# Last row pair of a token-mixing layer: an addition moved into the PSUM bank of C21, and the seven products in another order

## The chip, the cores and the metric

The kernel runs on one core of one Trainium2 chip. The time is the device time of one execution in microseconds; the number shown for a kernel is the median of its runs. A core has five engines with a queue each, which run side by side and wait for one another: TensorE (PE, matrix products, with its weight loads shown apart as PEld), VectorE (DVE), ScalarE (ACT), GpSimd (POOL) and SyncE (SP, here an issuer of transfers). Products go into PSUM, eight banks, and are read from there by VectorE or ScalarE.

## What is computed

A sum of three terms on a token matrix of 2048 rows and 640 columns: the input itself, the real part of a two-dimensional Fourier transform of its layer norm, and a token-mixing MLP on that layer norm, normalized once more.

```
xn = _layernorm(x, axis=-1)
return x + _A_ref(xn, A_dft_seq_re, A_dft_seq_im, A_dft_hid_re, A_dft_hid_im) + _B_ref(xn, B_w1, B_b1, B_w2, B_b2)

# _B_ref
h = _layernorm(x, axis=-1)                       # (B, S, D)
u = jnp.einsum("bsd,sf->bdf", h, w1) + b1        # (B, D, F)
u = _gelu(u)
y = jnp.einsum("bdf,fs->bds", u, w2) + b2        # (B, D, S)
```

S is 2048, D is 640, F is 1728. All is in float32. The change lies in the last 9 us, at the end of the product with w2, whose result is added to what the output rows hold already.

## The kernel before

**Stages.** The kernel runs through the Fourier product over the sequence (columns, TensorE lines 496 and 656), the product over the hidden dimension ("hid"), the first MLP product ("up0", "up1") and the second ("down0", "down1"). Every stage from "hid" on is made of row pairs, by `row_steps`. A row pair of "down1" computes output rows of tiles t and t + 8, each 128 x 640, over one half of F. The last is t = 7.

**Seven products.** A row pair is a 2 x 2 block product by seven products instead of eight (the Winograd form of Strassen's method). The weights' blocks A11, A12, A21, A22 and sums of them are the stationary operands; the other factor, already cut and summed, is the moving one, 320 columns wide. The sums are s = A21 + A22 (`first_sum`), then s - A11 (`s2`), A21 = A11 - A21 (`s3`), A12 = A12 - s (`s4`), all on VectorE (lines 877 and 149). P1 takes A11, P5 takes s as first summed, P6 takes s after s2, P2 takes A12, P7 takes A21 after s3, P3 takes A12 after s4, P4 takes A22. The results are C11 = P1 + P2, C12 = P1 + P6 + P5 + P3, C22 = P1 + P6 + P7 + P5 and C21 = P1 + P6 + P7 + P4. PSUM bank z holds the running sum P1, P1 + P6, P1 + P6 + P7; bank y holds P5, P5 + P3; bank w holds P2. In other row pairs P4 too accumulates in z. In the last one before the change it gets a bank of its own, u.

**Three matmuls for one.** An operand is cut into a high half, rounded to float32r by ScalarE (line 143, tile `piece`), and the rest, the low half, which VectorE computes (line 146). `three` (lines 151 to 157) issues high x high, high x low and low x high, so line 157 is the first to need the low half. In "down1" a product has three blocks of 128; P2, P3 and P4 are "stacked": their last block has only 64 rows, its low half lies in the other 64, and it takes two matmuls. Such a product has 8 matmuls, the others 9. A stacked low half is two VectorE operations. `fourth` (line 996, ScalarE) copies the 64 rows of A12 anew after s4 has changed them. The cut pieces lie in three buffers by turns, so the high half of a product waits until the product three places before has been done.

**Order.** Each engine's queue is in the order of the program. Turn i (`turn_of`) issues: loads, `reads` (the readers of the product of turn i - 1), `sums`, the high half of step i + 2, `extras`, the low half of step i + 2, `behind_lo`, and last the products of step i. So in a queue the reader of a product stands at the start of the next turn, behind all that earlier turns put there. A reader on VectorE adds the bank to the tile c (lines 952 and 961); P1's is a copy on ScalarE (line 965). Waits between engines on the same tile or bank are placed by the framework.

**The last row pair.** `base` is there: the old output rows are loaded beforehand into a tile (line 1136), VectorE adds them (lines 961, 978, 982, and what P4's reader finds in c), and the results go out by plain transfers (`each`, line 1128), on SP's queue and, for C21's right half, on ScalarE's. Other row pairs add to the output by GpSimd transfers (line 1038). Before the change P3's reader is followed by C11 plus its old output, P7's reader by c = z + old output of C21, and P4's reader adds bank u to that in two halves of 160 columns, both on VectorE, each sent as soon as it is done.

Of the kernel before, what the change touches and what calls it, by code (L numbers as in the profile page):

```python
# [11 lines left out]
AF = mybir.ActivationFunctionType  # L12
# [15 lines left out]
H2 = D // 2  # L28
# [42 lines left out]
def fnet_plus_mixer(  # L71
# [30 lines left out]
    nc = tc.nc  # L102
# [45 lines left out]
    def sub(to, a, b):  # L148
        nc.vector.tensor_sub(to, a, b)  # L149
# [20 lines left out]
    loads, sums, reads, extras, timed, behind_lo = (defaultdict(list) for _ in range(6))  # L170
# [683 lines left out]
    def row_steps(stage, nq, load_piece, at, end, bias=(None, None), base=None, earliest=0, each=None, aside={}, tail=False, stacked=()):  # L854
# [6 lines left out]
        s0, n = len(steps), nq * P  # L861
        raw, banks, held = {}, {}, {}
# [19 lines left out]

        order = (1, 5, 2, 6, 3, 7, 4) if base else (1, 5, 6, 2, 7, 3, 4)

        early = n < D
        loads_of = {-6: ("A11", "A21", "A22"), -4: ("A12",)} if early else {
# [9 lines left out]
        bank_of = {1: "z", 6: "z", 7: "z", 4: "z", 5: "y", 3: "y", 2: "w"}  # L898
        new_bank = (1, 5, 2)
        if tail:  # L900
            bank_of.update({5: "u", 7: "v", 4: "v"})
            new_bank += (7, 3)
        if base:
            bank_of[4] = "u"
            new_bank += (4,)
        of_moving = {1: 0, 2: 1, 3: 2, 5: 3, 7: 4, 4: 5, 6: 6}

        goes_to = {1: (0, 0, True), 5: (1, 1, True), 6: (0, 1, True), 2: (0, 0, False), 7: (1, 1, False),
# [16 lines left out]
        def read(i):  # L925
            def run():
                if i == 1:
                    held["c"] = place[at]()
                row, half, fresh = goes_to[i]
                cols = slice(half * H2, (half + 1) * H2)  # L930
                c, b = held["c"][:, row, cols], banks[bank_of[i]][:, :H2]
                if tail and i in (5, 7, 4):

                    def upper():
                        aside[i](row, half, b)
                        if i == 4:
                            end(held["c"])


                    if i == 7:  # L940
                        upper()
                    else:
                        extras[s0 + (4 if i == 5 else order.index(i) + 1)].append(upper)
                    if i == 5:
                        nc.scalar.activation(c, b, AF.Copy)
                    else:
                        nc.vector.tensor_add(c[:TAIL], b[:TAIL], c[:TAIL])
                    return
                if i in aside:
                    aside[i](row, half, b)  # L950
                elif not fresh:
                    nc.vector.tensor_add(c, b, c)  # L952
                elif base and i == 4:

                    for k, queue in enumerate((nc.sync, nc.scalar)):
                        of = slice(k * H2 // 2, (k + 1) * H2 // 2)
                        nc.vector.tensor_add(c[:, of], b[:, of], c[:, of])  # L957
                        each(c, row, half, True, of, queue)
                    return
                elif base and i != 1:  # L960
                    nc.vector.tensor_add(c, b, base()[:, row, cols])
                elif bias[row] is not None:
                    nc.scalar.activation(c, b, AF.Identity, bias=bias[row])
                else:
                    nc.scalar.activation(c, b, AF.Copy)  # L965
                if tail and i == 6:

                    low_row = held["c"][:, 1, :]
                    nc.vector.tensor_add(low_row[:, H2:], b, low_row[:, H2:])
                    extras[s0 + 3].append(lambda: nc.scalar.activation(low_row[:, :H2], b, AF.Copy))  # L970
                    p5 = banks["u"][:TAIL, :H2]
                    behind_lo[s0 + 3].append(lambda: nc.vector.tensor_add(c[:TAIL], p5, c[:TAIL]))
                if each:
                    each(c, row, half, i in (7, 3, 4))
                if base and i == 3:

                    c11 = held["c"][:, 0, :H2]
                    nc.vector.tensor_add(c11, c11, base()[:, 0, :H2])
                    each(c11, 0, 0, True)
                if base and i == 7:  # L980

                    nc.vector.tensor_add(held["c"][:, 1, :H2], b, base()[:, 1, :H2])
                if i == 4 and not each:
                    end(held["c"])
            return run
# [16 lines left out]
        if n == D or stacked:  # L1002

            operand[6] = "s"
            s2 = lambda: sub(raw["s"], raw["s"], raw["A11"])
            s3 = lambda: sub(raw["A21"], raw["A11"], raw["A21"])
            s4 = lambda: sub(raw["A12"], raw["A12"], raw["s"])
            if base:
                sums_of = {-2: (first_sum,)}
                behind_lo[s0 - 1].append(s2)  # L1010
                behind_lo[s0].extend((s4, s3))
                behind_lo[s0 + 1].append(fourth)
            elif stacked:
                sums_of = {-2: (first_sum,), 2: (s4,)}
                behind_lo[s0 - 1].append(s2)
                extras[s0].append(s3)
            elif s0 == s_hid:

                behind_lo[s0 - 2].append(first_sum)
                sums_of = {0: (s2,), 1: (s3,), 2: (s4,)}  # L1020
            else:
                sums_of = {-1: (s3,), 2: (s4,)}
                behind_lo[s0 - 2].append(first_sum)
                behind_lo[s0 - 1].append(s2)
        elif stage == "down0":

            sums_of[-2] = sums_of[-2][:1]
            behind_lo[s0 - 2].append(lambda: sub(raw["A21"], raw["A11"], raw["A21"]))
# [11 lines left out]
    def hidden(n, t, earliest):  # L1040
        ts = (t, t + 4)

        def load_piece(to, i, j):
            c, b = divmod(ts[i], CH // P)
            nc.sync.dma_start(to.rearrange("p (j t) -> p j t", j=ND), y_part[j][c][:, :, b * P : (b + 1) * P])

        return row_steps("hid", ND, load_piece, ("ca", "cb")[n % 2], lambda c: collect(c, ts), earliest=earliest)

    def up(stage, r, at):
# [60 lines left out]
        if tail:  # L1110
            aside += (5, 7, 4)
        s0 = row_steps(
            f"up{stage}", 4, load_piece, at, end, earliest=s_up - 4, aside={i: by_dram(i) for i in aside}, tail=tail,
        )
        return s0

    def down(stage, t, at):
        f0, nq = (0, 4) if stage == 0 else (4, 3)
        ts = (t, t + NS // 2)
        last = stage == 1 and t == NS // 2 - 1  # L1120

        def load_piece(to, i, j):
            f = f0 + NF2 * j
            nc.sync.dma_start(to, w2[ts[i], :, f * P : (f + nq) * P])

        def each(c, row, half, whole, at=slice(0, H2), queue=nc.sync):
            if whole:
                queue.dma_start(out_rows[ts[row]][:, half * H2 : (half + 1) * H2][:, at], c[:, at])

        held = []  # L1130

        def before():

            held.append(place["v"]())
            for i in range(2):
                nc.sync.dma_start(held[0][:, i, :], out_rows[ts[i]])

        if last:
            loads[len(steps) - LOADS].append(before)
        bias = [b2_sb[:, i : i + 1] if stage == 0 else None for i in ts]  # L1140
        return row_steps(
            f"down{stage}", nq, load_piece, at, lambda c: collect(c, ts), bias, (lambda: held[0]) if last else None,
            each=each if last else None, stacked=(2, 3, 4) if stage else (),
        )
# [27 lines left out]
    for t in range(NS):  # L1172
        parts = 2 if t < 6 else 1
        for i in range(parts):
            of = slice(i * P // parts, (i + 1) * P // parts)
# [69 lines left out]
    with tc.manual_schedule():  # L1245
        for word in START.split():
            start[word[0]](*map(int, word[1:].split("-")))
        for i in range(FIRST_STEP, len(steps) + 1):
# [6 lines left out]
            elif i >= s_hid:  # L1255
                k = sum(i >= s for s in (s_up, s_up + 7 * NF2, s_down))
                at, of = LONG_AT[k]
# [43 lines left out]
```

## Time and profile before

| | |
|---|---|
| time, median of 3 runs | 864.93 us (864.7 to 864.96) |
| span of the profiled execution | 862.9 us |
| TensorE busy | 858.4 us (99%) |
| VectorE busy | 696.6 us (81%) |
| ScalarE busy | 529.1 us (61%) |
| granted TensorE clock up to the last matmul | 1.00 |

The profile is of one execution, whose times count from its first instruction. In a timeline a row gives the start, the duration, the engine, the line of the kernel, the operation, out<-in by tile names, the shape, and "xN" where N like rows that follow one another were merged; in brackets stands how long the engine stood idle before it, and what ended that. "SPq" and "ACTq" are transfers being issued by these queues. TensorE's rows are starts of matmuls that overlap: one starts every 0.15 us and each takes 0.31 us to its end.

### The profile page before, as it was taken

How to read it: one execution, taken by the hardware profiler on the slowest of the kernel's cores; microseconds unless marked ns; L12 is line 12 of the kernel's file. 1: busy time of each engine (PE TensorE's matmuls, PEld its weight loads, DVE VectorE, ACT ScalarE, POOL GpSimd, SP SyncE). 2: the span in 40 equal slices, each digit the busy share in tenths (PEclk: the TensorE clock that was granted, in tenths of full speed). 3: DMA queues.
4: the chain of work that ended last, by engine and by line, in shares of the span. 5: the costliest groups of instructions: out<-in, count | busy, mean ns of one | idle time of the engine just before them, and what ended most of it. 6: DMA issues, size and time to landing. Idle time of an engine off the chain costs nothing.

```text
span 862.9 us, 13981 instructions
## 1 busy us (share of the span) xinstructions
PE 858.4 (99%) x4883; PEld 786.5 (91%) x4883; DVE 696.6 (81%) x1172; ACT 529.1 (61%) x987; POOL 179.7 (21%) x249
## 2 busy tenths in 40 slices
PE   9999999999999999999999999999999999999998
PEld 6888888888888888889999999999999999999998
DVE  7998868784757888877887788888678978897887
ACT  7766676755445555657565556676577856555654
POOL 5333222212121211122100101111312321101211
PEclk9999999999999999999999999999999999999999
DMA  8889594989593746779576766664688779766786
GB/s 316 287 223 322 126 298 130 246 196 297 139 262 61 200 97 144 171 128 211 122 170 169 159 147 181 196 180 152 148 178 186 169 213 243 184 139 130 157 167 149
DMA packets 93350, 159.44 MB, mean 185 GB/s; under 512 B 9408, under 2 KB 37824, under 8 KB 92928
## 3 DMA queue, kind: packets, MB, share of 16 engines
q0 software_dynamic: 26432, 60.40, 38.4%
q1 hardware_dynamic: 66704, 98.06, 35.3%
q8 instruction: 38, 0.62, 0.3%
q14 instruction: 32, 0.26, 0.1%
q10 hardware_dynamic: 144, 0.08, 0.0%
HBM read 102.05 MB, written 61.70 MB: 190 GB/s over the span
## 4 chain that ended last, share of the span: by engine, by line
PE 99%; DMA 0%; SPq 0%; ACT 0%; DVE 0%; issue 0%; DVEq 0%
PE psum L656 44%; PE psum L155 18%; PE psum L154 18%; PE psum L157 17%; PE psum L496 2%; DMA pieces<-in_dft_seq 0%; SPq L520 0%; ACT piece L143 0%; DVE pair L957 0%; DVEq L1297 0%
## 5 line engine op out<-in xcount | busy, mean ns | idle before, releaser
L146 DVE TENSOR_TENSOR piece<-pieces,piece 128x512 fp32r<-128x512 f32 (+4 forms) x514 | 338.7, 660 | 138.6 <-ACT piece L143 135.3
L143 ACT ACTIVATE piece<-pieces 128x512 fp32r<-128x512 f32 (+3 forms) x490 | 306.5, 626 | 230.8 <-PE psum L656 98.1
L656 PE MATMUL psum<-piece,n 128*128 128x512 f32 x1656 | 376.9, 389 | 0.0
L656 PEld LDWEIGHTS psum<-piece,n 128*128 128x128 f32 x1656 | 310.6, 188 | 65.1 <-DVE piece L146 0.4
L155 PE MATMUL psum<-sup,piece 128*128 128x320 f32 x392 | 120.8, 309 | 0.0
L154 PE MATMUL psum<-sup,piece 128*128 128x320 f32 x392 | 120.8, 309 | 0.0
L155 PE MATMUL psum<-sdown,piece 128*128 128x320 f32 x392 | 120.8, 309 | 0.0
L154 PE MATMUL psum<-sdown,piece 128*128 128x320 f32 x392 | 120.8, 309 | 0.0
L149 DVE TENSOR_TENSOR pieces<-pieces 128x512 f32<-128x512 f32 (+3 forms) x146 | 116.5, 803 | 2.8
L469 POOL DMA_DIRECT2D y<-c x76 | 65.5, 898 | 251.4 <-DVE c L692 132.4
L157 PE MATMUL psum<-sup,piece 128*128 128x320 f32 x368 | 113.7, 309 | 0.0
L157 PE MATMUL psum<-sdown,piece 128*128 128x320 f32 x368 | 113.7, 309 | 0.0
L157 PE MATMUL psum<-shid,piece 128*128 128x320 f32 x280 | 86.5, 309 | 0.0
L155 PE MATMUL psum<-shid,piece 128*128 128x320 f32 x280 | 86.5, 309 | 0.0
L154 PE MATMUL psum<-shid,piece 128*128 128x320 f32 x280 | 86.5, 309 | 0.0
L154 PEld LDWEIGHTS psum<-sup,piece 128*128 128x128 f32 x392 | 73.6, 188 | 0.0
L155 PEld LDWEIGHTS psum<-sdown,piece 128*128 128x128 f32 x392 | 73.6, 188 | 0.0
L155 PEld LDWEIGHTS psum<-sup,piece 128*128 128x128 f32 x392 | 73.6, 188 | 0.0
L154 PEld LDWEIGHTS psum<-sdown,piece 128*128 128x128 f32 x392 | 73.6, 188 | 0.0
L1038 POOL DMA_DIRECT2D out<-pair x38 | 33.0, 942 | 189.0 <-DVE pair L952 157.3
L965 ACT ACTIVATE pair<-psum 128x320 f32<-128x320 f32 x101 | 44.0, 436 | 42.4 <-PE psum L157 39.3
L157 PEld LDWEIGHTS psum<-sup,piece 128*128 128x128 f32 x368 | 69.1, 188 | 0.0
(120 smaller groups left out, 863.7 us busy)
## 6 DMA issues: line engine op xcount, KB each, us to landing
pieces<-in_dft_seq SPq DMA_DIRECT2D x136, 256.0 KB, 5.5
y<-c POOLq DMA_DIRECT2D x106, 256.0 KB, 6.1
pieces<-in_w SPq DMA_DIRECT2D x88, 256.0 KB, 4.0
out<-pair POOLq DMA_DIRECT2D x38, 320.0 KB, 5.3
pieces<-y SPq DMA_DIRECT2D x32, 320.0 KB, 4.2
pieces<-in_w SPq DMA_DIRECT2D x32, 192.0 KB, 3.0
up<-pair POOLq DMA_DIRECT2D x8, 640.0 KB, 3.4
pair<-in_x SPq DMA_DIRECT2D x12, 320.0 KB, 4.7
```

Of the source, the lines that this page charges most:

```text
L143: nc.scalar.activation(hi, src, AF.Copy)
L146: nc.vector.tensor_sub(lo, src, hi.bitcast(F32))
L149: nc.vector.tensor_sub(to, a, b)
L154: nc.tensor.matmul(psum, wh, mh, start=first, stop=False, skip_group_check=True)
L155: nc.tensor.matmul(psum, wh, ml, start=False, stop=last and wl is None, skip_group_check=True)
L157: nc.tensor.matmul(psum, wl, mh, start=False, stop=last, skip_group_check=True)
L469: nc.gpsimd.dma_start(y_part[m][c][:, j, :], t, accum_op=ALU.add)
L496: nc.tensor.matmul(to, (hi, hi, lo)[k], w[k % 2], start=k == 0 and i == 0, stop=k == 2 and i % 4 == 3, skip_group_check=True,)
L656: nc.tensor.matmul(to, (hi, hi, lo)[k], w[k % 2], start=k == 0 and begin, stop=k == 2 and q == 3, skip_group_check=True,)
L965: nc.scalar.activation(c, b, AF.Copy)
L1038: nc.gpsimd.dma_start(out_rows[ts[i]], c[:, i, :], accum_op=ALU.add)
```

## The change

The order of the products of the last row pair becomes P1, P5, P6, P7, P2, P3, P4. P4 has no bank of its own: it accumulates in z, to which VectorE has added the old output of C21 (`tensor_add(b, b, base)`, in PSUM) behind P7's reader. P4's reader is two copies of bank z into c: the right half on ScalarE, the left on VectorE, then a transfer of each. C11 gets its old output behind P6's reader and goes out behind P2's; C12 goes out behind P3's, C22 behind P7's. s3 stands alone behind the low half that turn s0 makes, now P6's; s4 and `fourth` move from turns s0 and s0 + 1 to turn s0 + 2, behind the low half of P2.

```diff
-        order = (1, 5, 2, 6, 3, 7, 4) if base else (1, 5, 6, 2, 7, 3, 4)
+        order = (1, 5, 6, 7, 2, 3, 4) if base else (1, 5, 6, 2, 7, 3, 4)
...
-        if base:
-            bank_of[4] = "u"
-            new_bank += (4,)
...
                 elif base and i == 4:
 
-                    for k, queue in enumerate((nc.sync, nc.scalar)):
-                        of = slice(k * H2 // 2, (k + 1) * H2 // 2)
-                        nc.vector.tensor_add(c[:, of], b[:, of], c[:, of])
-                        each(c, row, half, True, of, queue)
+                    left, right = (slice(k * H2 // 2, (k + 1) * H2 // 2) for k in range(2))
+                    nc.scalar.activation(c[:, right], b[:, right], AF.Copy)
+                    nc.vector.tensor_copy(c[:, left], b[:, left])
+                    each(c, row, half, True, left, nc.sync)
+                    each(c, row, half, True, right, nc.scalar)
                     return
...
                 if each:
-                    each(c, row, half, i in (7, 3, 4))
-                if base and i == 3:
+                    each(c, row, half, i in (7, 2, 3))
+                if base and i == 6:
 
                     c11 = held["c"][:, 0, :H2]
                     nc.vector.tensor_add(c11, c11, base()[:, 0, :H2])
-                    each(c11, 0, 0, True)
                 if base and i == 7:
 
-                    nc.vector.tensor_add(held["c"][:, 1, :H2], b, base()[:, 1, :H2])
+                    nc.vector.tensor_add(b, b, base()[:, 1, :H2])
...
                 behind_lo[s0 - 1].append(s2)
-                behind_lo[s0].extend((s4, s3))
-                behind_lo[s0 + 1].append(fourth)
+                behind_lo[s0].append(s3)
+                behind_lo[s0 + 2].extend((s4, fourth))
```

## Prediction

> **What bounds the kernel now.** I read the page first (span, busy times, chain that ended last), then the timelines of the last row pair engine by engine.
>
> ```profile
> span 862.9 us, 13981 instructions
> PE 99%; DMA 0%; SPq 0%; ACT 0%; DVE 0%; issue 0%; DVEq 0%
> ```
>
> TensorE is the chain for 99% of the span. The profiled execution spans 862.9 us; the median of the runs is 864.93, so 2.03 us lie around the span, and I carry that offset over. A change at the end pays only in time during which TensorE stands still, or in the tail behind its last matmul. The next fence has TensorE's first and last matmul of the row pair (60 in all), the last two output transfers, and where a transfer lands.
>
> ```profile
> 850.65 0.31 PE L154 MATMUL psum<-sdown,piece 128*128 128x320 f32 x1
> 859.30 0.31 PE L155 MATMUL psum<-sdown,piece 128*128 128x320 f32 x1
> ...
> 860.00 0.33 SPq L1128 DMA_DIRECT2D out<-pair  x1
> 860.23 0.37 ACTq L1128 DMA_DIRECT2D out<-pair  x1
> ...
> out<-pair ACTq DMA_DIRECT2D x1, 80.0 KB, 1.6
> ```
>
> Sixty starts in 8.65 us are one each 0.1466 us, without a gap. P1, P5, P6, P7 have 9 matmuls (1.32 us), the stacked P2, P3, P4 have 8 (1.17 us). Before, the starts are P1 850.65, P5 851.97, P2 853.29, P6 854.46, P3 855.78, P7 856.95, P4 858.27; the last matmul ends at 859.61. VectorE, from s2 = s - A11 on:
>
> ```profile
> 851.37 0.56 DVE L149 TENSOR_TENSOR pieces<-pieces 128x384 f32<-128x384 f32 x1
> 851.96 0.73 DVE L146 TENSOR_TENSOR piece<-pieces,piece 64x128 fp32r<-64x128 f32 x2
> 852.73 1.02 DVE L149 TENSOR_TENSOR pieces<-pieces 128x384 f32<-128x384 f32 x2
> 853.67 0.55 DVE L146 TENSOR_TENSOR piece<-pieces,piece 128x384 fp32r<-128x384 f32 x1
> 854.14 0.48 DVE L961 TENSOR_TENSOR pair<-psum,pair 128x320 f32<-128x320 f32 x1
> 854.65 0.73 DVE L146 TENSOR_TENSOR piece<-pieces,piece 64x128 fp32r<-64x128 f32 x2
> 855.30 0.48 DVE L952 TENSOR_TENSOR pair<-psum,pair 128x320 f32<-128x320 f32 x1
> 855.70 0.55 DVE L146 TENSOR_TENSOR piece<-pieces,piece 128x384 fp32r<-128x384 f32 x1
> 856.16 0.48 DVE L961 TENSOR_TENSOR pair<-psum,pair 128x320 f32<-128x320 f32 x1
> 856.68 0.73 DVE L146 TENSOR_TENSOR piece<-pieces,piece 64x128 fp32r<-64x128 f32 x2
> 857.32 0.48 DVE L952 TENSOR_TENSOR pair<-psum,pair 128x320 f32<-128x320 f32 x1
> 857.72 0.48 DVE L978 TENSOR_TENSOR pair<-pair 128x320 f32<-128x320 f32 x1
> 858.48 0.49 DVE L952 TENSOR_TENSOR pair<-psum,pair 128x320 f32<-128x320 f32 x1 [0.27 <-PE psum L157]
> 858.88 0.48 DVE L982 TENSOR_TENSOR pair<-psum,pair 128x320 f32<-128x320 f32 x1
> 859.65 0.55 DVE L957 TENSOR_TENSOR pair<-psum,pair 128x160 f32<-128x160 f32 x2 [0.28 <-PE psum L155]
> ```
>
> VectorE works without a pause from 851.37 to 858.20, so its queue, not its speed, decides when a bank has been read. An independent successor starts 0.08 us before an operation's end (the cut at 853.67 takes 0.55, the next starts at 854.14); the stacked cut, or one that waits for its predecessor, starts 0.03 after it. P6 ends about 855.94, its reader (L961) runs 856.16 to 856.64, and P7, which accumulates in the same bank z, starts at 856.95: P3 covers the reading.
>
> **The change part by part.** In the new order P7 follows P6 directly, in the same bank, and P6's sum must have been read before P7 adds to it. The new starts would be P6 853.29, P7 854.61 if nothing waited. Ahead of P6's reader in VectorE's queue stand now: low P6, s3, low P7, reader of P5, low P2, s4. Two of these wait for ScalarE's high halves, and those for VectorE's s2 and s3. The row pair before shows such a hand-over:
>
> ```profile
> 842.57 1.03 DVE L149 TENSOR_TENSOR pieces<-pieces 128x384 f32<-128x384 f32 x2
> 843.78 0.56 DVE L146 TENSOR_TENSOR piece<-pieces,piece 128x384 fp32r<-128x384 f32 x1 [0.18 <-ACT piece L143]
> ...
> 843.23 0.53 ACT L143 ACTIVATE piece<-pieces 128x384 fp32r<-128x384 f32 x1 [0.74 <-DVE pieces L149]
> ```
>
> ScalarE starts 0.11 after s2's end (842.57 + 0.55 = 843.12), takes 0.53, and VectorE starts 0.02 later: 0.66 from end to start, during which there s3 ran. Here s3 stands behind low P6, and nothing fills either gap. ScalarE's own queue:
>
> ```profile
> 852.17 0.44 ACT L965 ACTIVATE pair<-psum 128x320 f32<-128x320 f32 x1 [0.47 <-PE psum L157]
> ...
> 853.32 0.31 ACT L996 ACTIVATE pieces<-pieces 64x128 f32<-64x128 f32 x1 [0.30 <-DVE pieces L149]
> ...
> 855.98 0.53 ACT L143 ACTIVATE piece<-pieces 128x384 fp32r<-128x384 f32 x1 [0.80 <-PE psum L157]
> ```
>
> Step by step: s2 ends 851.93 as before. High P6 852.04 to 852.57; low P6 852.59 to 853.14, in time for P6. s3 853.06 to 853.61. High P7 853.72 to 854.25; low P7 854.27 to 854.82. Reader of P5 854.74 to 855.22. Low P2 855.25 to 855.98. s4 856.02 to 856.57. Reader of P6 856.49 to 856.97. TensorE's answer to VectorE in such a wait is on no row here; between the hand-overs above (0.02 and 0.11) I take 0.08. **P7 starts at 857.05 in place of 854.61: TensorE stands 2.44 us.** That is the main term. P7's other inputs were ready at 854.82, so the reader alone sets it.
>
> Behind it nothing is late again. P2 starts 858.37, P3 859.54, P4 860.72. The fourth quarter's copy (L996) waits for s4 and runs 856.6 to 856.9, high P3 to 857.5, low P3 (behind L978, moved from P3's turn to P6's) ends 858.23: 1.3 us early. The readers of P7 and the addition into the bank (two VectorE operations, like L952 and L982) follow P7's end: 858.57 to 859.45. A VectorE write into PSUM is on no row. Between 0.28 (one of L957's pair, half the columns) and 0.96 (L982 twice, should the bank be slower to write than to read) I take L982's own 0.48, the same operation with another target; low P4 then ends about 860.25, 0.47 before P4. At 0.96 it would end 860.73, where P4's third matmul, the first that uses it, is due at 861.01: either end hides. High P4 needs P7's buffer, free at P7's end as L143 at 855.98 was at P6's, and runs beside the two. The transfers of C11 and C12 move later on SP's queue (P2's and P3's readers, about 860.7 and 861.4), C22's earlier; the last of them is issued a microsecond ahead of C21's. Without the stall's cover, low P4 would be the next thing late.
>
> The tail: the last matmul ends 859.61 + 2.44 = 862.05. ScalarE's half (128x160 from PSUM: L996 takes 0.31 for 128 columns, L965 0.44 for 320) I take at 0.31, VectorE's copy at L957's 0.31. Do the two halves run side by side? This row pattern from another stage speaks against it:
>
> ```profile
> 600.33 0.44 ACT L965 ACTIVATE pair<-psum 128x320 f32<-128x320 f32 x1 [1.02 <-PE psum L157]
> 600.80 0.49 DVE L969 TENSOR_TENSOR pair<-psum,pair 128x320 f32<-128x320 f32 x1 [0.66 <-ACT pair L965]
> 601.32 0.44 ACT L970 ACTIVATE pair<-psum 128x320 f32<-128x320 f32 x1
> ```
>
> L969 and L965 read the same bank and write different places, yet VectorE stood 0.66 us until ScalarE had ended (600.77), and L970 again began only at L969's end (601.29). So I take the halves one after the other: ScalarE 862.09 to 862.40, VectorE 862.42 to 862.73, the last issue on SP at 862.76 against 860.23 before: +2.53, where side by side it would be 862.43, +2.20. The Trainium skill, "PSUM — Partial Sum Buffer", section "PSUM bank collisions raise a hardware error", says that no two engines may access one bank and quadrant at once, two reads included; by that rule the sum is the +2.53, and the trace agrees with its 0.66.
>
> Sum: 2.44 stall + 0.09 in the tail = +2.53. Span 862.9 + 2.53 = 865.4; time 864.93 + 2.53 = **867.5** (+0.29%). Its own range, with 0.2 either way for the hand-overs and 0.33 less for halves side by side: 866.9 to 867.9.
>
> **The rivals.** *VectorE doesn't lose its two waits (ends on the other side: not slower).* Were the high halves of P6 and P7 ready when VectorE reaches them, both gaps of 0.66 would go: P6 read by 855.65, P7 at 855.73, stall 1.12; with the tail in turn (+0.09) 866.1, side by side (-0.24) 865.8, both within 0.2%. It decides as soon as 0.8 us of the 2.53 go. For it: ScalarE is idle enough. Against: s2 and s3 are inputs of those cuts.
>
> *P7 doesn't wait for P6's reader, or the reader comes right at P6's end (the reordering costs nothing).* Then P3 is first late (high P3 ends 857.5 against a start at 857.1, low P3 858.23), and behind low P3 stand the reader of P7, the addition and low P4, which ends 859.85: P4's third matmul at 859.93 against 858.56, +1.37 there and +0.09 in the tail, 866.4. Only if these cuts came early too would the tail's -0.24 be left, 864.7. Against: an accumulation over an unread sum would change C12.
>
> *The clock falls in the pause.* The windows view behind the last matmul:
>
> ```profile
> core 0: us, PE busy (x) PEld busy (x) DVE busy (x) ACT busy (x) POOL busy (x), PEclk, DMA share, GB/s
> 859.60:862.00 2.40, 0.01 (x1) 0.00 (x0) 0.55 (x2) 0.00 (x0) 0.00 (x0) 1.00 0.44 144
> ...
> 862.20:862.40 0.20, 0.00 (x0) 0.00 (x0) 0.00 (x0) 0.00 (x0) 0.00 (x0) 0.66 0.00 0
> ```
>
> PEclk is the granted clock: 0.66 in a 0.2 us stretch is full speed for a third of it, so it falls to half at about 862.26, 2.65 us after TensorE's end; the new pause (854.77 to 857.05) is 2.28. The 33 matmuls behind it take 4.84 us, so half speed throughout would add 4.84 (872.3), through P7 alone 1.32 (868.8). The Trainium skill, "TensorE: Matmul & The Clock Gate", section "Part 1: The HAM clock gate", puts the fall behind an idle window of about 3.4 us that runs freely; by it a pause of 2.28 seldom suffices. The trace's fall at 2.65 us is earlier than that, so a chance stays.
>
> **How the numbers follow.** Forecast 0.70; waits not lost 0.08; no wait on the reader 0.09; clock 0.10; faster for some unseen reason 0.03. About 0.2%, 1.73 us, is what a measurement of this kernel can tell from no change. Slower: 0.70 less a little for a shorter pause, plus 0.10, is 0.77; same 0.20; faster 0.03. Range: 866.0 to 868.8, which takes in the forecast, the first rival with its tail in turn, the second without early cuts, and the clock down through P7; left out are the cheaper ends of both rivals, a longer fall of the clock and the unseen gain, some 0.18.
>
> **What would show it.** TensorE idle once, about 2.4 us, just ahead of P7's first matmul, ended by VectorE's reader of P6 (L961); VectorE idle about 0.66 twice, ahead of low P6 and low P7, ended by ScalarE; granted clock 1.00 to the last matmul; no idle before P2, P3, P4; VectorE's final copy starting at ScalarE's end. Wrong: no TensorE gap, a gap before P3 or P4, or P6's reader ahead of low P2.

## Result, and the profile after

The changed kernel takes 869.02 us (median of 5, 868.9 to 871.08) against 864.70 (median of 5): ratio 1.0053, interval 1.0041 to 1.0065. It is slower by 0.53%. The forecast was 867.5, with a range up to 868.8; the way was right, the size too small, and the time lies outside the range.

From the page of the changed kernel, and then from its TensorE timeline, the end of P6, the start of P7, and the matmuls behind it:

```profile
span 867.1 us, 13980 instructions
```

```profile
854.65 0.31 PE L157 MATMUL psum<-sdown,piece 128*128 128x320 f32 x1
857.30 0.39 PE L154 MATMUL psum<-sdown,piece 128*128 128x320 f32 x1 [2.34 <-DVE pair L959]
...
858.11 0.43 PE L157 MATMUL psum<-sdown,piece 128*128 128x320 f32 x1
858.33 0.47 PE L154 MATMUL psum<-sdown,piece 128*128 128x320 f32 x1
858.60 0.47 PE L155 MATMUL psum<-sdown,piece 128*128 128x320 f32 x1
...
861.26 0.45 PE L154 MATMUL psum<-sdown,piece 128*128 128x320 f32 x1
861.53 0.33 PE L155 MATMUL psum<-sdown,piece 128*128 128x320 f32 x1
861.69 0.31 PE L157 MATMUL psum<-sdown,piece 128*128 128x320 f32 x1
...
863.59 0.31 PE L155 MATMUL psum<-sdown,piece 128*128 128x320 f32 x1
```

Two things cost time. TensorE stands 2.34 us ahead of P7 until VectorE's reader of P6 (now line 959) has ended. And from 858.2 to 861.5 its matmuls start every 0.27 us in place of 0.147. VectorE's rows up to that reader show why it comes so late:

```profile
851.57 0.56 DVE L149 TENSOR_TENSOR pieces<-pieces 128x384 f32<-128x384 f32 x1
852.78 0.56 DVE L146 TENSOR_TENSOR piece<-pieces,piece 128x384 fp32r<-128x384 f32 x1 [0.65 <-ACT piece L143]
853.25 0.55 DVE L149 TENSOR_TENSOR pieces<-pieces 128x384 f32<-128x384 f32 x1
854.46 0.56 DVE L146 TENSOR_TENSOR piece<-pieces,piece 128x384 fp32r<-128x384 f32 x1 [0.65 <-ACT piece L143]
854.93 0.48 DVE L959 TENSOR_TENSOR pair<-psum,pair 128x320 f32<-128x320 f32 x1
855.43 0.73 DVE L146 TENSOR_TENSOR piece<-pieces,piece 64x128 fp32r<-64x128 f32 x2
856.20 0.56 DVE L149 TENSOR_TENSOR pieces<-pieces 128x384 f32<-128x384 f32 x1
856.67 0.48 DVE L959 TENSOR_TENSOR pair<-psum,pair 128x320 f32<-128x320 f32 x1
```

Row for row this is the queue that the prediction wrote down: s2, low P6, s3, low P7, reader of P5, low P2, s4, reader of P6, with two waits of 0.65 for ScalarE. The windows view (us, then busy time of each engine, then the granted clock third from the end) shows the second loss as one of the clock:

```profile
857.00:858.00 1.00, 0.70 (x5) 0.73 (x6) 0.86 (x4) 0.62 (x2) 0.00 (x0) 1.00 0.11 20
858.00:859.00 1.00, 1.00 (x6) 1.00 (x6) 0.41 (x1) 0.00 (x0) 0.00 (x0) 0.57 0.00 0
859.00:860.00 1.00, 1.00 (x6) 1.00 (x5) 0.63 (x2) 0.53 (x1) 0.00 (x0) 0.50 0.00 0
860.00:861.00 1.00, 1.00 (x6) 1.00 (x5) 0.96 (x3) 0.00 (x0) 0.00 (x0) 0.50 0.24 88
861.00:862.00 1.00, 1.00 (x7) 1.00 (x7) 0.52 (x2) 0.00 (x0) 0.00 (x0) 0.73 0.22 76
```

The clock falls to half at 858.14 (0.57 over a microsecond is full speed for 0.14 of it), 0.84 us after TensorE had started again, and comes back at 861.55. The tail, from ScalarE's, VectorE's and SP's timelines:

```profile
863.94 0.30 ACT L953 ACTIVATE pair<-psum 128x160 f32<-128x160 f32 x1 [4.04 <-PE psum L155]
...
864.27 0.33 DVE L954 COPY pair<-psum 128x160 f32<-128x160 f32 x1 [1.02 <-ACT pair L953]
...
864.63 0.33 SPq L1125 DMA_DIRECT2D out<-pair  x1
```

The two copies of one bank run one after the other; VectorE, idle for 1.02 us, begins at ScalarE's end.

**Where the 4.3 us between the two spans are.** P1 starts 0.19 later in this execution (850.84 against 850.65), which is spread between executions. P7, 27 matmuls on, was due at 850.84 + 27 x 0.1466 = 854.80 and starts at 857.30: 2.50. From P7's start to the last start are 6.29 us in place of 32 x 0.1466 = 4.69: 1.60. From the last start to the end of the span (867.13 and 862.86 in the traces, before rounding) are 3.54 in place of 3.56: -0.02. Sum: 0.19 + 2.50 + 1.60 - 0.02 = 4.27, all of 867.13 - 862.86.

### The profile page after: what moved, and what is told of

It reads as the page before. It is cut to its first block, busy times and chain, and to the rows that moved or that the text cites. A ratio compares the mean times of both kernels' runs of the same rounds, so it can differ in the third digit from the quotient of the medians.

```text
span 867.1 us, 13980 instructions
## 1 busy us (share of the span) xinstructions
PE 859.9 (99%) x4883; PEld 788.1 (91%) x4883; DVE 696.9 (80%) x1171; ACT 529.2 (61%) x988; POOL 179.2 (21%) x249
## 4 chain that ended last, share of the span: by engine, by line
PE 98%; DVE 1%; DMA 0%; issue 0%; ACT 0%; SPq 0%; DVEq 0%; ACTq 0%
PE psum L656 43%; PE psum L154 18%; PE psum L155 18%; PE psum L157 17%; PE psum L496 2%; DMA pieces<-in_dft_seq 0%; DVE piece L146 0%; ACT piece L143 0%; DVE pair L949 0%; DVE pieces L149 0%; DVE pair L959 0%; SPq L520 0%; DVE pieces L877 0%; DVE pair L954 0%; ACT pair L953 0%
## 5 line engine op out<-in xcount | busy, mean ns | idle before, releaser
L154 PEld LDWEIGHTS psum<-sdown,piece 128*128 128x128 f32 x392 | 74.3, 189 | 2.6 <-ACT pieces L993 2.6
L155 PEld LDWEIGHTS psum<-sdown,piece 128*128 128x128 f32 x392 | 74.3, 190 | 0.0
L154 PEld LDWEIGHTS psum<-sup,piece 128*128 128x128 f32 x392 | 73.6, 188 | 0.0
L155 PEld LDWEIGHTS psum<-sup,piece 128*128 128x128 f32 x392 | 73.6, 188 | 0.0
L157 PEld LDWEIGHTS psum<-sdown,piece 128*128 128x128 f32 x368 | 69.5, 189 | 0.0
```

What stands on the lines that cost most here:

```text
L154: nc.tensor.matmul(psum, wh, mh, start=first, stop=False, skip_group_check=True)
L155: nc.tensor.matmul(psum, wh, ml, start=False, stop=last and wl is None, skip_group_check=True)
L157: nc.tensor.matmul(psum, wl, mh, start=False, stop=last, skip_group_check=True)
```

## Experiments

Theory 1: P7 waits for P6's reader at the end of VectorE's queue (2.5 us), and this pause lowers TensorE's clock (1.6 us). Theory 2: the matmuls are slow for what VectorE and ScalarE do beside them. Theory 3: the loss comes from the addition into PSUM and P4's wait for it. In the table TensorE's pause is counted from the end of one matmul to the start of the next; the delay of a product, from start to start, is 0.16 us longer. The times:

| run | median us (runs) | before, same chip | ratio, interval | TensorE's pause in the profile |
|---|---|---|---|---|
| fill14 | 867.42 (9) | 864.81 | 1.0030, 1.0020 to 1.0040 | 0.29 |
| order_only | 868.60 (4) | 864.81 | 1.0045, 1.0029 to 1.0060 | 2.34 |
| bank_only | 866.59 (10) | 864.81 | 1.0020, 1.0011 to 1.0030 | 1.04 and 0.40 |
| s3_first_s4_later | 866.07 (10) | 864.81 | 1.0015, 1.0006 to 1.0024 | 0.81 |
| s3_first | 866.85 (10) | 864.88 | 1.0020, 1.0010 to 1.0029 | 1.40 |
| fill7 | 867.84 (10) | 864.88 | 1.0037, 1.0027 to 1.0047 | 1.31 |
| order_fill14 | 867.38 (9) | 864.88 | 1.0025, 1.0016 to 1.0035 | 0.29 |
| bank_tuned | 865.17 (10) | 864.88 | 1.0005, 0.9996 to 1.0014 | 0.00 and 0.10 |
| fill3 | 869.40 (4) | 865.15 | 1.0044, 1.0029 to 1.0059 | 1.90 |
| after_again | 868.08 (8) | 865.15 | 1.0038, 1.0024 to 1.0052 | 2.34 |

**fill14: the pause filled.** Behind P6's products:

```diff
+                if base and i == 6:
+                    spare = psum[(bank_turn[0] + 3) % 8][:, :H2]
+                    for k in range(14):
+                        nc.tensor.matmul(
+                            spare, w[0][:, k % nq * P : (k % nq + 1) * P], moving[stage, k % nq][:, 0, of_moving[i], :],
+                            start=k == 0, stop=k == 13, skip_group_check=True,
+                        )
```

> Theory 1 (the wait for P6's reader costs about 2.5 us, and TensorE's pause of 2.3 us lowers its clock for one more loss of about 1.6 us): 14 matmuls of P6's own operands into a spare bank, never read, fill 2.05 us of the pause and move nothing else; granted clock 1.00 throughout, time about 2.5 us above before, 867.2 to 867.5. Theory 2 (the slow matmuls behind the pause come from VectorE's and ScalarE's accesses there, not from the pause): still 13 slow matmuls, 868.8 to 869.2.

867.42, granted clock 1.00 in every run. TensorE's rows:

```profile
855.23 2.21 PE L923 MATMUL psum<-sdown,piece 128*128 128x320 f32 x14
857.73 0.39 PE L154 MATMUL psum<-sdown,piece 128*128 128x320 f32 x1 [0.29 <-DVE pair L966]
857.96 0.31 PE L155 MATMUL psum<-sdown,piece 128*128 128x320 f32 x1
```

The fillers take the place in which P7 was due, and P7 starts 857.73 - 855.23 = 2.50 us later, as without them. VectorE's and ScalarE's work is the same, and the slow matmuls are gone. Theory 2 falls: the 1.6 us go with the clock, and the clock stays up when the pause is filled.

**order_only: the order without the bank.** The changed kernel with P4's bank of its own, the old output of C21 added outside PSUM, and the old tail:

```diff
+        if base:
+            bank_of[4] = "u"
+            new_bank += (4,)
...
-                    nc.vector.tensor_add(b, b, base()[:, 1, :H2])
+                    nc.vector.tensor_add(held["c"][:, 1, :H2], b, base()[:, 1, :H2])
```

> The new order of products with P4 in a bank of its own and the old tail (two additions on VectorE). Theory 1 (all of the loss is the order, P7 right behind P6 in one bank): as the changed kernel, 868.8 to 869.2. Theory 3 (the loss comes from VectorE's addition into PSUM, from P4 waiting for it, or from the two copies): 864.7 to 865.5.

868.60, with the same 2.34 us of pause ahead of P7. The four runs had a mean granted clock of 0.998 (868.79, 868.41), 0.996 (870.51) and 1.00 (867.20); one stretch of 3.41 us at half speed takes 0.002 off the mean of an execution. So the order alone brings the loss, and one run whose clock stayed up lies at the forecast.

**bank_only: the bank without the order.**

```diff
-        order = (1, 5, 6, 7, 2, 3, 4) if base else (1, 5, 6, 2, 7, 3, 4)
+        order = (1, 5, 6, 2, 7, 3, 4)
...
-                behind_lo[s0 + 2].extend((s4, fourth))
+                behind_lo[s0 + 1].extend((s4, fourth))
```

> The addition into the bank, P4 accumulating on it and the two copies, with the order of the other row pairs (P1, P5, P6, P2, P7, P3, P4), in which P2 stands between P6 and P7. Theory 1: no pause of TensorE over 0.3 us, time within 0.5 us of before. Theory 3: 868 to 869.

A miss: 866.59, 1.78 above before. TensorE paused twice:

```profile
856.49 0.38 PE L154 MATMUL psum<-sdown,piece 128*128 128x320 f32 x1 [1.04 <-DVE pair L959]
...
859.61 0.38 PE L154 MATMUL psum<-sdown,piece 128*128 128x320 f32 x1 [0.40 <-DVE psum L979]
```

P7 was due at 855.28 and starts 1.21 later; P4 was due at 859.05 and starts 0.56 later. With P2 in between, P6's reader is still late, since low P7 stands ahead of it and waits for ScalarE, whose queue has the fourth copy first (L993, from 854.49 to 854.80). VectorE's rows, with low P7 and P6's reader, then low P4, P7's reader and the addition into the bank:

```profile
855.38 0.56 DVE L146 TENSOR_TENSOR piece<-pieces,piece 128x384 fp32r<-128x384 f32 x1 [0.53 <-ACT piece L143]
855.86 0.48 DVE L959 TENSOR_TENSOR pair<-psum,pair 128x320 f32<-128x320 f32 x1
...
857.93 0.73 DVE L146 TENSOR_TENSOR piece<-pieces,piece 64x128 fp32r<-64x128 f32 x2
858.58 0.48 DVE L949 TENSOR_TENSOR pair<-psum,pair 128x320 f32<-128x320 f32 x1
858.98 0.49 DVE L979 TENSOR_TENSOR psum<-psum,pair 128x320 f32<-128x320 f32 x1
```

Here the addition does hold P4: P7 ends at 858.04, its reader stands behind low P4 until 858.58, and only P3 lies between P7 and P4. In the changed kernel P2 and P3 lie there, and the addition ends well before P4's start, by 1.24 us in the profile of after_again and by 0.54 in that of s3_first_s4_later, where the pause is 0.81. So theory 3 names a real cost, but not the one that was paid.

**s3_first_s4_later and s3_first: the queue ahead of the reader.** The first has both lines of this edit, the second only the first:

```diff
-                behind_lo[s0].append(s3)
-                behind_lo[s0 + 2].extend((s4, fourth))
+                extras[s0].append(s3)
+                sums_of[3] = (s4, fourth)
```

> The changed kernel with s3 ahead of low P6 and with s4 and the fourth copy behind P6's reader. Theory 1 (VectorE's queue ahead of the reader sets the pause): one of the two waits for ScalarE is filled by s3, s4's 0.47 is gone; P7's delay falls from 2.5 to about 1.0 us. With full clock 865.7; if even this pause lowers the clock, 867.2. If the queue is not what sets it: 869.

> The changed kernel with s3 ahead of low P6 alone. By VectorE's queue as measured: the first wait for ScalarE is filled by s3 and the second shortens to 0.2; P7's delay falls from 2.50 to about 1.55 us, TensorE's pause to 1.4. Theory A (any pause of that order lowers the clock): 867.9 and a granted clock of 0.998. Theory B (the clock needs a longer pause, the 0.8 us of the run with s4 later did nothing): 866.4, clock 1.00.

In the profiles P7 is 0.97 us late with both lines (due at 854.35) and 1.56 late with the first, against 2.50:

```profile
855.32 0.38 PE L154 MATMUL psum<-sdown,piece 128*128 128x320 f32 x1 [0.81 <-DVE pair L959]
```

```profile
855.91 0.38 PE L154 MATMUL psum<-sdown,piece 128*128 128x320 f32 x1 [1.40 <-DVE pair L959]
```

Both are the sums that VectorE's queue gives (1.0 and 1.55). The clock stayed at 0.999 or 1.00 in all 20 runs. The medians, 1.26 and 1.97 above before, are 0.3 to 0.4 more than the delays; runs with an undisturbed clock spread by 1.9 us in each of the two, and the profiled ones, 865.58 and 866.09, are near the low ends.

**fill7 and fill3: how long a pause the clock bears.** fill14 with 7 and with 3 matmuls.

> The changed kernel with 7 matmuls of P6's own operands into a spare bank, never read: P7's delay stays 2.5 us, TensorE's pause is 1.3 us. Theory A: as the changed kernel, about 869, clock 0.998. Theory B: as with 14, 867.4, clock 1.00. Some runs of each would say that the pause's place against a free-running window decides.

> The changed kernel with 3 matmuls of P6's own operands into a spare bank, never read: P7's delay stays 2.5 us, TensorE's pause is 1.9 us, between the 1.4 that left the clock alone and the 2.34 that lowered it. If a length between decides sharply: all runs about 869 or all 867.4. If the pause's place against a window of 3.4 us decides, in which a share of idle time is needed: some runs at clock 0.998 and about 869, others at 1.00 and about 867.4.

With 1.31 us of pause the clock stayed at 0.999 or 1.00 in all ten runs (median 867.84), so "any pause" is wrong. One of these runs took 870.39 at a clock of 1.00: a long time alone is no sign of a lowered clock. With 1.90 us it fell in all four (0.998, 869.21 to 869.53). By what was expected this speaks for a sharp length and against windows; after_again, below, speaks for windows. The windows view of fill3, whose pause runs from 855.84 to 857.74:

```profile
857.50:858.00 0.50, 0.26 (x2) 0.29 (x3) 0.49 (x2) 0.47 (x2) 0.00 (x0) 1.00 0.32 56
858.00:858.50 0.50, 0.50 (x5) 0.50 (x5) 0.36 (x2) 0.09 (x1) 0.00 (x0) 0.85 0.09 15
858.50:859.00 0.50, 0.50 (x4) 0.50 (x3) 0.35 (x1) 0.00 (x0) 0.00 (x0) 0.50 0.00 0
```

It falls at 858.35, 0.6 us after the pause had ended.

**after_again: the changed kernel once more.**

> The changed kernel unaltered, beside it on the same chip. Most runs at clock 0.998 and 868.9 to 869.2; those at 1.00, if any, near 867.4, those at 0.996 near 871: steps of about 1.6 to 2 us by the number of lowered windows.

Partly a miss: most runs kept their clock. Five of eight were at 1.00 and took 867.08 to 868.42, two at 0.998 took 869.30 and 869.41, one at 0.996 took 871.10. The profiled execution (span 865.7) is one of the five, with the same pause:

```profile
857.34 0.39 PE L154 MATMUL psum<-sdown,piece 128*128 128x320 f32 x1 [2.34 <-DVE pair L959]
857.56 0.31 PE L155 MATMUL psum<-sdown,piece 128*128 128x320 f32 x1
```

```profile
858.00:858.50 0.50, 0.50 (x6) 0.50 (x5) 0.43 (x2) 0.00 (x0) 0.00 (x0) 1.00 0.00 0
```

So one and the same pause lowered the clock in one execution and not in another.

**order_fill14: order and bank apart, with a steady clock.** order_only with fill14's matmuls.

> The new order alone (P4 in its own bank, old tail) with the 14 filling matmuls, so that the clock can't blur it. If the bank part of the change (addition into PSUM, P4 on it, two copies) costs or gains nothing behind the pause: the time of the changed kernel with the same filling, 867.4, within 0.3 us. If the bank part costs: below 867.0. If its tail gains: above 867.7.

867.38 against 867.42 for fill14: behind the pause the bank part neither costs nor gains anything that can be measured.

**bank_tuned: the bank part at its best.** bank_only's order, with

```diff
+                    if base and i == 2:
+                        nc.vector.tensor_add(c, c, base()[:, 0, :H2])
...
-                if base and i == 6:
-
-                    c11 = held["c"][:, 0, :H2]
-                    nc.vector.tensor_add(c11, c11, base()[:, 0, :H2])
...
-                behind_lo[s0].append(s3)
+                extras[s0].append(s3)
...
-            reads[s0 + e + 1].append(read(i))
+            (behind_lo[s0 + 5] if base and i == 2 else reads[s0 + e + 1]).append(read(i))
```

> The bank part of the change in the order P1, P5, P6, P2, P7, P3, P4, with s3 first, s4 behind low P7, and C11's two additions behind the addition into the bank. Between P7's end and P4's start lie a reader of 0.40, the addition of 0.49 and two hand-overs of 0.2 together, 1.1 us, against P3's 1.17 of cover less the 0.16 by which P7's last result follows its last start. Expected: P6's reader delays P7 by 0.1 or less, P4 waits 0.1 to 0.4, time 864.9 to 865.3; a version below 864.6 would beat the kernel before. If the queue is late again, 866 or more.

865.17 against 864.88, ratio 1.0005 with an interval across 1, from 0.3 us less to 1.2 us more. In the profile P7 starts 0.16 us late and P4 0.26, each with a second matmul that is late as well:

```profile
855.11 0.31 PE L155 MATMUL psum<-sdown,piece 128*128 128x320 f32 x1
855.42 0.38 PE L154 MATMUL psum<-sdown,piece 128*128 128x320 f32 x1
...
857.83 0.31 PE L155 MATMUL psum<-sdown,piece 128*128 128x320 f32 x1
858.24 0.39 PE L154 MATMUL psum<-sdown,piece 128*128 128x320 f32 x1
```

From the first start of the row pair (850.12) to the last (859.34) are 9.22 us, against 8.65 before, and the last issue comes 1.04 us behind the last start, against 0.93: the tail is no shorter. So even here the bank gains nothing and costs TensorE 0.57 us in the profile, which the runs are too few to tell from nothing. No version here beats the kernel before.

## Why the prediction was wrong in size

- **The stall ahead of P7: right.** Predicted 2.44 us of delay by the reader of P6; measured 2.50. The two gaps of 0.66 were 0.65, the reader started at 856.67 (856.49 predicted, plus the 0.19 by which the execution was later). The hand-over from VectorE to TensorE took 0.15 (857.15 to 857.30), for which 0.08 had been taken. s3_first and s3_first_s4_later moved the delay by what the queue's sum says.
- **Nothing late behind it: right.** No pause before P2, P3 or P4. The addition into PSUM took 0.49 (L979), 0.48 had been taken. That low P4 would be the next thing late without the stall is borne out in part: in s3_first_s4_later, with 0.97 us of the delay left, low P4 ends at 859.27, 0.08 before the third matmul of P4 starts. P4's wait in bank_only doesn't show it, since P2 stands elsewhere there.
- **The tail: nearly right.** The copies ran in turn, and the last issue came 1.04 us after the last matmul's start, 0.93 before: +0.11, for +0.09. Yet the span ended 0.02 earlier behind that start, since what follows the last issue was 0.13 us shorter; why stays open. The rule of the Trainium skill, "PSUM — Partial Sum Buffer", section "PSUM bank collisions raise a hardware error", that no two engines may access one bank at once, agrees with the trace, in which VectorE stands until ScalarE's end (864.24) and starts at 864.27. What would come of two readers at once no run here shows.
- **The clock: the step that failed.** The rival "the clock falls in the pause" got 0.10, because the clock before had fallen 2.65 us after the last matmul and the pause was 2.28, read as a delay that the pause wouldn't reach. So the sum, 2.44 + 0.09, has no term for the clock. It fell in all five runs of the comparison. Its price was put at 1.32 for P7 alone; one stretch of half speed lasts 3.41 us (858.14 to 861.55) and cost 1.60, of which 0.07 is the late second matmul of P7. Forecast plus that price is 869.1. In executions whose clock stayed up (five of after_again, one of order_only) the time is 867.1 to 868.4, around the forecast.
- **The range: a slip, and chance.** 0.2 us either way on 867.46 gives 867.7 at the upper end of the sum's own range, not 867.9; the stated range doesn't hang on it. And that the time lies outside it is in part chance: the same kernel has a median of 868.08 in the eight runs of after_again, inside the range, because five of them kept their clock.

**What the 2.65 us were.** The windows view of order_only, whose pause runs from 854.89 to 857.23:

```profile
856.90:857.00 0.10, 0.00 (x0) 0.00 (x0) 0.10 (x2) 0.10 (x1) 0.00 (x0) 0.99 0.54 102
857.00:857.10 0.10, 0.00 (x0) 0.00 (x0) 0.10 (x2) 0.07 (x2) 0.00 (x0) 0.50 0.15 26
```

The falls fit a count over windows of 3.41 us, one behind the other, that lie differently in each execution. In this trace the clock comes back at 860.41 and falls again behind the end, at 867.24 (0.70 in a tenth of a microsecond is full speed for 0.04 of it):

```profile
860.40:860.50 0.10, 0.10 (x2) 0.10 (x1) 0.10 (x2) 0.10 (x1) 0.00 (x0) 0.94 0.00 0
867.20:867.30 0.10, 0.00 (x0) 0.00 (x0) 0.00 (x0) 0.00 (x0) 0.00 (x0) 0.70 0.00 0
```

That is 3.41 and 6.83 us on, one window and two. The changed kernel has 858.14, 861.55 and 868.38, and fill3 858.35, 861.76 and 868.59: the same distances. So one change of the clock shows where the windows of its execution lie. The time in them without a matmul, by TensorE's rows:

| profile | window | idle in it, us | clock at its end |
|---|---|---|---|
| after_again | 852.60 to 856.02 | 1.02 | stays |
| after_again | 856.02 to 859.43 | 1.32 | stays |
| s3_first | 852.53 to 855.94 | 1.40 | stays |
| s3_first, around its last matmul | 859.35 to 862.77 | 1.79 | stays |
| fill3 | 854.94 to 858.35 | 1.90 | falls |
| order_only | 853.59 to 857.00 | 2.11 | falls |
| changed kernel | 854.72 to 858.14 | 2.34 | falls |
| kernel before, around its last matmul | 858.85 to 862.26 | 2.65 | falls |

In the last five windows of all twelve profiles, none with 1.79 us or less lowered the clock and each with 1.90 or more did. The 2.65 us were thus no delay: they were the idle part of the window that ended there. The profile of after_again is the test of this. Its clock falls at 866.26, behind the end:

```profile
866.00:867.00 1.00, 0.00 (x0) 0.00 (x0) 0.00 (x0) 0.00 (x0) 0.00 (x0) 0.63 0.00 0
```

Counted back by 3.41 us, an edge lies at 856.02 and cuts the pause of 2.34 into 1.02 and 1.32, each below the need. An estimate from these numbers: with windows placed at random, such an edge keeps the clock up in some 40% of executions ((2 x 1.79 - 2.34) / 3.41 to (2 x 1.90 - 2.34) / 3.41), and so 5 of 5 lowered was partly luck; it was 11 of 17 over all runs with this pause. A pause of 1.90 should lower it in about half, so the four of four of fill3 are more than expected, and four runs don't decide it. Open as well: three of the 17 runs had a clock of 0.996, as if two stretches had been lowered, and the kernel before, which has no such pause, had 0.998 or 0.997 in three of the 65 runs beside the experiments (866.52 to 866.63), too few to account for 11 of 17.

## What to carry to other kernels

Before two products that accumulate in one bank are set side by side, look for who must read the bank in between and write down all that stands ahead of that reader in its engine's queue, with every wait in it. A pause of TensorE has a second price: ask how much of it falls into one window of the clock's count, not how long after the last matmul the clock once fell. Where the median of a few runs depends on such a window, look at the granted clock of each run before reading a step in the time.

## What the runs showed of the hardware

- A pause of 1.90 us lowered TensorE's granted clock to 0.50 in four of four runs, one of 2.34 in 11 of 17 (changed kernel 5 of 5, order_only 3 of 4, after_again 3 of 8), those up to 1.40 in none of 40; a run without a profile counts as lowered when its mean clock is 0.998 or less. The lowered stretch lasts 3.41 us; it began inside the pause in the profile of order_only and 0.84 us after its end in that of the changed kernel. In the profiles a window of 3.41 us with 1.90 us of idle or more ended in a fall, one with 1.79 did not. The Trainium skill, "TensorE: Matmul & The Clock Gate", section "Part 1: The HAM clock gate", puts the fall behind an idle window of about 3.4 us; the window's length agrees with the 3.41 here, but 1.90 us of idle in it were enough.
- At a granted clock of 0.50 the 128x320 matmuls started every 0.266 us, at 1.00 every 0.147: a ratio of 1.82, not 2.
- The first matmul behind a wait was followed by the next after 0.22 us in place of 0.147 (857.30 to 857.52; 0.23 in fill14, 857.73 to 857.96), so a wait cost TensorE 0.07 to 0.08 us beyond the wait.
